# Three weight conversions placed behind the store of the last but one token tile on ScalarE

## The chip, the core and the metric

The kernel runs on one core of a Trainium2 chip. The metric is the device time of one launch in microseconds (us). A core has five engines with an instruction stream each: TensorE (PE, matrix products), VectorE (DVE), ScalarE (ACT), GpSimd (POOL) and SyncE (SP, which here only starts transfers). Each stream is worked off in its own order; an instruction that waits holds up all that stand behind it on its engine. ACT and POOL start transfers as well: ACT stores of plain tiles, POOL gathers and scatters whose rows are named by an index tile.

## The reference, cut to what matters

```python
attn = softmax(masked q k^T) v                  # 2 batches, 8 heads, 768 positions, 64 wide
x  = attn as [1536 tokens, 512]
x2 = ((x @ w_a) * (x @ w_b)) @ w_out            # w_a, w_b [512, 1536], w_out [1536, 512]
logits = x2 @ w_gate                            # 8 experts, 192 tokens each, picked greedily
for e in range(8):
    out[tokens of e] = maximum(x2[tokens of e] @ w1[e], 0) @ w2[e]   # w1 [512, 1024], w2 [1024, 512]
```

## The kernel before

The kernel runs in four stages. Attention comes first, then the gated product G = (x w_a)(x w_b), then x2 = G w_out together with the choice of experts, and then the eight experts one after the other. Matrix products in full precision are made of high and low parts: a value is rounded into a tile `hi` (or `gh`, `ehi`, `xt`), the rest goes into `lo` (`gl`, `elo`), and the products hi·hi, hi·lo and lo·hi are added.

The change sits at the seam between x2 and the experts. `second` makes x2 in 12 tiles of 128 tokens (t = 0 to 11), each from three units of four rows of blocks of G, so 36 units. For a unit, ACT rounds a piece of G into `gh` (L977), POOL subtracts into `gl` (L978), and PE makes twelve products into `px` (L992). There are three buffers of `gh`, so the rounding of unit i + 3 waits until PE is through with unit i. After the third unit of a tile ACT copies `px` into `x2` (L998) and starts its store into the DRAM tensor `x2d` (L999); the last tile (t = 11) is copied into `x2last`.

PE's order is written out by hand in this stage (a `manual_schedule` of PE alone); that of ACT, DVE, POOL and SP is chosen by the scheduler of the framework, and is fixed in the program. In the experts' stage the orders of PE, ACT and DVE are written by hand.

Expert 0 needs its 192 rows of x2. `first_rows` has POOL gather them from `x2d` with two indirect transfers into `first0` (128 rows) and `first1` (64 rows, both L1033). They read the tiles 0 to 10 of `x2d` only; rows of tile 11 come out of `x2last`. PE turns the gathered rows (`begin_rows`, L1050, eight matmuls for each of the two) and adds the rows of tile 11 by a product of `x2last` with a selection tile `ones` (L1162, eight matmuls). ACT and DVE split the result `pt` into the high and low `xt` (L1084, L1085), and the first products `p` of expert 0 follow (L1107, 64 matmuls, then the second products `y`, from L1113 on).

The experts' weights come in 64 chunks of 512 KB (`eraw`, loaded by SP at L1012). `weight_high` rounds a chunk on ACT into `ehi` (L1017) and `weight_low` subtracts on DVE into `elo` (L1022). Chunks 0 to 3 are loaded and converted ahead of the experts. Chunk 0 goes into a pool of its own; chunks 1, 2 and 3 go into a pool, `pre2`, that takes over the room of the routing's tiles, and so its first conversion waits for the routing's last instruction on DVE (`oidx`, L947). Chunks 4 and later go into a pool that takes over the room of the x2 stage.

Of the kernel before, what the change touches and what calls it, by code (L numbers as in the profile page):

```python
# [63 lines left out]
def f32(ap):  # L64
    return ap.bitcast(F32)


class Kernel:
# [500 lines left out]
    def run(self):  # L569
        tc, nc = self.tc, self.nc  # L570
        H, NT, E = self.H, self.NT, self.E
        with ExitStack() as top:
# [107 lines left out]
            def gate(Q, c):  # L680
                assert all(f in done for f in range(4 * Q + 4))
                for j in range(4):
                    f = 4 * Q + j
                    nc.tensor.matmul(pg[c][32 * j:32 * j + 32, :], wp[:, f, :], g_of(f, 512 * c, 512),
                                     start=(Q == 0), stop=(Q == 2), tile_position=(0, 32 * j),
                                     skip_group_check=True)
# [31 lines left out]
            exraw = exs.enter_context(tc.tile_pool(name="exraw", bufs=EXR, side="right"))  # L718
            pre = exs.enter_context(tc.tile_pool(name="pre", bufs=1, side="right"))
# [7 lines left out]
            with tc.manual_schedule(engines={mybir.EngineType.PE}):  # L727
                x2last = pre.tile([128, self.Dm], F32, name="x2last")
                rest = self.second(sec, g_parts, woh, wol, rpsum, x2last)
                left = [36 * NT]  # L730

                def fill(n):
                    for _ in range(n):
                        next(rest, None)
                        left[0] -= 1

                fill(START[0])
                gate(2, 2)
                for c in range(3):
                    nc.scalar.activation(lgT[:, c, :], pg[c], AF.Copy)  # L740
                if "lgT" in self.dbg:
                    nc.sync.dma_start(self.dbg["lgT"], lgT)
                L = self.fold_logits(rpool, rpsum, lgT, fill)
                gpx.close()
                rpq = ExitStack()
                rpp = rpq.enter_context(tc.tile_pool(name="rpq", bufs=1, space=PSUM, side="right"))
                self.routing(rpool, rpsum, rpp, L, lgT.rearrange("p a (b c) -> p (a b) c", c=128), ROUNDS, False, fill)
                rpq.close()
                trp = exs.enter_context(tc.tile_pool(name="trp", bufs=1, space=PSUM, side="right"))
                fill(left[0] - 35)  # L750
                first = self.first_rows(pre, rpool, x2last)
                weights = []
                for c in range(4):
                    if c == 1:
                        rps.close()
                        pre2 = exs.enter_context(tc.tile_pool(name="pre2", bufs=1, side="right"))
                    weights.append(self.weight_high(pre2 if c else pre, self.weight_load(exraw, c), 3 if c else 1))
                    self.weight_low(weights[c])
                fill(10 ** 6)
                rows, last, ones = first  # L760
                pts = [trp.tile([128, 2, self.cap], F32, name="pt", tag="ptr", bufs=2) for _ in range(2)]
                for h in range(2):
                    for k in range(4):
                        self.begin_rows(pts[k // 2][:, k % 2, :], rows, h, k)
# [201 lines left out]
    def second(self, pool, g_parts, woh, wol, ps, x2last):  # L966

        nc = self.nc
        units = [(t, f0) for t in range(self.NT) for f0 in (0, 4, 8)]
        parts, out = {}, {}  # L970

        def split(i):
            t, f0 = units[i]
            gh = pool.tile([128, 4, 128], F32R, name="gh", tag="gh", bufs=3)
            gl = pool.tile([128, 4, 128], F32R, name="gl", tag="gl", bufs=3)
            for fs, src in g_parts(f0, 128 * t):
                nc.scalar.activation(gh[:, fs], src, AF.Copy)  # L977
                nc.gpsimd.tensor_tensor(gl[:, fs], src, f32(gh[:, fs]), op=OP.subtract)  # L978
            parts[i] = gh, gl

        split(0)
        split(1)
        for i, (t, f0) in enumerate(units):
            if i + 2 < len(units):
                split(i + 2)
            gh, gl = parts.pop(i)
            if f0 == 0:
                out[t] = ps.tile([128, 512], F32, name="px2", tag="px2", bufs=2)
            for ff in range(4):
                f = f0 + ff  # L990
                for w, x, n in ((gh, woh, 0), (gh, wol, 1), (gl, woh, 2)):
                    nc.tensor.matmul(out[t], w[:, ff, :], x[f], start=(f == 0 and n == 0), stop=(f == 11 and n == 2))  # L992
                    yield
            if f0 == 8:
                x2 = x2last
                if t + 1 < self.NT:
                    x2 = pool.tile([128, 512], F32, name="x2", tag="x2", bufs=1)
                nc.scalar.activation(x2, out.pop(t), AF.Copy)  # L998
                nc.scalar.dma_start(self.x2d[128 * t:128 * t + 128, :], x2)  # L999


    def weight_load(self, pool, c):
# [348 lines left out]
```

## Time and profile before

| what | value |
|---|---|
| device time, median of 3 runs | 632.42 us (631.93 to 633.57) |
| device time of the profiled execution | 632.53 us |
| span of the profiled execution | 630.5 us, so 2.0 us lie around it |
| mean granted clock of TensorE over the span | 0.989 |
| PE busy | 610.8 us (97%) |
| DVE, ACT, POOL busy | 403.4, 338.8, 177.6 us |

The span is what the profiler saw from the first instruction to the last. Busy times of different engines overlap. [...]

### The profile page before, as it was taken

The numbers are of one execution on the slowest core, as the hardware profiler recorded it, in microseconds if no ns is written. First come the engines' busy times: TensorE is split into PE (matmuls) and PEld (weight loads), VectorE is DVE, ScalarE is ACT, GpSimd is POOL, SyncE is SP. The second block draws the span as 40 slices with busy tenths as digits, with TensorE's granted clock in tenths as the row PEclk, the third lists the DMA queues.
The fourth block names the chain that finished last, engine by engine and source line by source line (L and its number), as shares of the span: only waits on it lengthen the run. The fifth ranks groups of instructions, "written<-read, shape, count | busy, mean of one in ns | idle before, by whom it ended". The sixth has DMA issues, their size and how long they took to land.

```text
span 630.5 us, 10136 instructions
## 1 busy us (share of the span) xinstructions
PE 610.8 (97%) x3645; PEld 479.6 (76%) x3645; DVE 403.4 (64%) x864; ACT 338.8 (54%) x672; POOL 177.6 (28%) x300
## 2 busy tenths in 40 slices
PE   7989999999999999999999999999989999999994
PEld 5667777788877878787867766677778888888883
DVE  6788876679975766431125557666327878778782
ACT  4888777635442433223126655764335866657661
POOL 5658565500000000001024343444421323122221
PEclk9999999999999999999999999999979999999997
DMA  7976320035541433200040000000186788777831
GB/s 159 213 156 150 68 69 2 2 98 170 165 136 34 135 99 101 67 1 0 1 125 25 18 35 18 31 21 19 39 286 190 253 262 270 246 251 223 272 135 34
DMA packets 82603, 72.16 MB, mean 114 GB/s; under 512 B 41073, under 2 KB 69745, under 8 KB 82545
## 3 DMA queue, kind: packets, MB, share of 16 engines
q1 hardware_dynamic: 78704, 61.99, 33.9%
q0 software_dynamic: 2112, 6.30, 3.3%
q10 hardware_dynamic: 1728, 3.15, 1.3%
q8 instruction: 31, 0.51, 0.3%
q14 instruction: 28, 0.22, 0.1%
HBM read 65.13 MB, written 6.29 MB: 113 GB/s over the span
## 4 chain that ended last, share of the span: by engine, by line
PE 81%; issue 9%; POOL 3%; DVE 2%; ACT 2%; DMA 2%; SPq 0%; POOLq 0%; DVEq 0%; ACTq 0%
PE pb L559 14%; PE pa L559 14%; PE px L992 14%; PE p L1107 7%; PE pa L470 4%; PE px L367 4%; PE s L273 3%; PE pa L334 3%; PE pq L871 2%; POOL out_dram L1122 2%; PE y L1113 1%; PE y L1114 1%; PE pt L237 1%; PE y L1118 1%; PE y L1115 1%
## 5 line engine op out<-in xcount | busy, mean ns | idle before, releaser
L1022 DVE TENSOR_TENSOR elo<-eraw,ehi 128x1024 fp32r<-128x1024 f32 x64 | 75.9, 1217 | 5.0 <-ACT ehi L1017 5.0
L1107 PE MATMUL p<-xt,ehi 128*128 128x384 f32 x256 | 73.6, 360 | 0.0
L978 POOL TENSOR_TENSOR gl<-G,gh 128x512 fp32r<-128x512 f32 (+1 forms) x40 | 49.5, 1248 | 68.2 <-ACT gh L977 64.2
L1017 ACT ACTIVATE ehi<-eraw 128x1024 fp32r<-128x1024 f32 x64 | 65.0, 1054 | 3.7 <-DVE oidx L947 2.2
L1107 PE MATMUL p<-xt,elo 128*128 128x192 f32 x256 | 64.7, 254 | 0.0
L992 PE MATMUL px<-woh,gh 128*128 128x512 f32 x144 | 59.5, 413 | 0.0
L279 ACT ACTIVATE A<-sm,negmax 128x264 f32<-128x264 f32 (+1 forms) x96 | 46.9, 490 | 22.3 <-DVE negmax L277 21.2
L978 POOL TENSOR_TENSOR gl<-GE,gh 128x256 fp32r<-128x256 f32 x8 | 7.1, 883 | 182.0 <-ACT gh L977 178.5
L860 DVE TENSOR_SCALAR gt<-lgT,vmax 128x1536 bf16<-128x1536 f32 x40 | 45.5, 1199 | 20.1 <-ACT lgT L835 17.7
L992 PE MATMUL px<-woh,gl 128*128 128x512 f32 x144 | 57.2, 397 | 0.0
L992 PE MATMUL px<-wol,gh 128*128 128x512 f32 x144 | 57.0, 396 | 0.0
L301 POOL TENSOR_SCALAR A<-A,rs 128x256 f32<-128x256 f32 (+1 forms) x96 | 43.2, 469 | 43.5 <-DVE rs L288 23.9
L566 DVE TENSOR_TENSOR G<-asb,pb 128x512 f32<-128x512 f32 x32 | 21.9, 685 | 48.0 <-PE pb L559 48.0
L559 PE MATMUL pb<-xh,whi 128*128 128x512 f32 x128 | 51.7, 404 | 0.0
L1122 POOL DMA_INDIRECT out_dram<-o,oidx x16 | 26.3, 1645 | 90.1 <-ACT o L1131 68.1
L559 PE MATMUL pb<-xh,wlo 128*128 128x512 f32 x128 | 50.1, 392 | 0.0
L559 PE MATMUL pa<-xh,wlo 128*128 128x512 f32 x128 | 50.0, 390 | 0.0
L559 PE MATMUL pb<-xl,whi 128*128 128x512 f32 x128 | 49.9, 390 | 0.0
L559 PE MATMUL pa<-xl,whi 128*128 128x512 f32 x128 | 49.9, 390 | 0.0
L559 PE MATMUL pa<-xh,whi 128*128 128x512 f32 x128 | 49.8, 389 | 0.0
L1107 PEld LDWEIGHTS p<-xt,elo 128*128 128x128 f32 x256 | 49.4, 193 | 0.6 <-ACT xt L1084 0.2
L1107 PEld LDWEIGHTS p<-xt,ehi 128*128 128x128 f32 x256 | 48.3, 189 | 0.7
(224 smaller groups left out, 1418.5 us busy)
## 6 DMA issues: line engine op xcount, KB each, us to landing
eraw<-in_moe_w_dram SPq DMA_DIRECT2D x64, 512.0 KB
wraw<-in_moe_w_a_dram SPq DMA_DIRECT2D x12, 512.0 KB
wraw<-in_moe_w_b_dram SPq DMA_DIRECT2D x12, 512.0 KB
wraw<-in_moe_w_out_dram SPq DMA_DIRECT2D x12, 512.0 KB
x2d<-x ACTq DMA_DIRECT2D x11, 256.0 KB
rawv<-in_v_dram SPq DMA_DIRECT2D x10, 256.0 KB
rawq<-in_q_dram SPq DMA_DIRECT2D x8, 256.0 KB
rawk<-in_k_dram SPq DMA_DIRECT2D x8, 256.0 KB
```

Of the source, the lines that this page charges most:

```text
L279: nc.scalar.activation(st.A2[:, j, h, c0:], sm[:, :n], AF.Exp, bias=self.negmax[:, cc], scale=-1.0, accum_out=self.sums[:, cc])
L301: nc.gpsimd.tensor_scalar(blocks, blocks, st.r2[:, j, h:h + 1], 1.0, op0=OP.mult, op1=OP.mult)
L367: nc.tensor.matmul(px[64 * h:64 * h + 64, cols], vv[:, vcol[h]], st.AT[h][:, sl].rearrange("p a b -> p (a b)"), start=(not g and n == 0), ...
L470: nc.tensor.matmul(p, w[:, k, :], x[c][:, k, :], start=(k == 0 and t == 0), stop=(k == 3 and t == 2))
L559: nc.tensor.matmul(pab[m], w[:, k, :], x[:, k, :], start=(k == 0 and t == 0), stop=(k == 3 and t == 2))
L860: nc.vector.tensor_scalar(gt, vrow, v, None, op0=OP.is_lt)
L978: nc.gpsimd.tensor_tensor(gl[:, fs], src, f32(gh[:, fs]), op=OP.subtract)
L992: nc.tensor.matmul(out[t], w[:, ff, :], x[f], start=(f == 0 and n == 0), stop=(f == 11 and n == 2))
L1017: self.nc.scalar.activation(hi, raw, AF.Copy)
L1022: (eng or self.nc.vector).tensor_tensor(lo, raw, f32(hi), op=OP.subtract)
L1107: nc.tensor.matmul(p1[:, ff, 0:c], w[:, k, cols], x[:, k, 0:c], start=(n == 0), stop=(k == 3), skip_group_check=True)
L1122: st = nc.gpsimd.indirect_dma_start(out=self.out, out_offset=bass.IndirectOffsetOnAxis(ap=self.oidx[:n, 2 * e + h:2 * e + h + 1], axis=0), ...
```

## The change

`second` keeps the instruction that starts the store of a tile; when chunks 1, 2 and 3 are converted, the name `x2store` holds the store of tile 10, the last but one (tile 11 is made after them by `fill(10 ** 6)`). `issue_after` gives each instruction that the block writes on that instruction's engine, which is ACT, a place behind it. It orders them on the engine and adds no wait. The loads of the chunks and the subtractions on DVE are outside of the block.

```diff
                     if c == 1:
                         rps.close()
                         pre2 = exs.enter_context(tc.tile_pool(name="pre2", bufs=1, side="right"))
-                    weights.append(self.weight_high(pre2 if c else pre, self.weight_load(exraw, c), 3 if c else 1))
+                    raw = self.weight_load(exraw, c)
+
+                    with tc.issue_after(self.x2store.ins) if c else ExitStack():
+                        weights.append(self.weight_high(pre2 if c else pre, raw, 3 if c else 1))
                     self.weight_low(weights[c])
...
                 nc.scalar.activation(x2, out.pop(t), AF.Copy)
-                nc.scalar.dma_start(self.x2d[128 * t:128 * t + 128, :], x2)
+                self.x2store = nc.scalar.dma_start(self.x2d[128 * t:128 * t + 128, :], x2)
```

On ACT, at the end of the x2 stage, the rows before are these. `x_4985` is the copy of tile 9 and `x_5072` that of tile 10, the first pair of `gh` after tile 9's store is the first unit of tile 11, and the names in brackets are the engines and transfers that a row waits for.

```order
L999 DMA x2d<-x_4985 128x512 [waits Activation_49]
L977 ACTIVATE gh<-G 128x256 [waits PE_49,Pool_49]
L977 ACTIVATE gh<-G 128x256
L977 ACTIVATE gh<-G 128x512 [waits PE_49,Pool_49]
L1017 ACTIVATE ehi<-eraw 128x1024 [waits DVE_49,PE_49]
L1017 ACTIVATE ehi<-eraw 128x1024 x2
L977 ACTIVATE gh<-G 128x512 [waits PE_49,Pool_49]
L998 ACTIVATE x_5072<-px_4992 128x512 [waits DMAHW2_49,PE_49]
L999 DMA x2d<-x_5072 128x512 [waits Activation_49]
L998 ACTIVATE x2last<-px_5079 128x512 [waits PE_49]
L999 DMA x2d<-x2last 128x512 [waits Activation_49]
```

At the same place of the changed program, whose lines stand three higher from here on:

```order
L1002 DMA x2d<-x_4985 128x512 [waits Activation_49]
L980 ACTIVATE gh<-G 128x256 [waits PE_49,Pool_49]
L980 ACTIVATE gh<-G 128x256
L980 ACTIVATE gh<-G 128x512 [waits PE_49,Pool_49] x2
L1001 ACTIVATE x_5072<-px_4992 128x512 [waits DMAHW2_49,PE_49]
L1002 DMA x2d<-x_5072 128x512 [waits Activation_49]
L1020 ACTIVATE ehi<-eraw 128x1024 [waits DVE_49]
L1020 ACTIVATE ehi<-eraw 128x1024 x2
L1001 ACTIVATE x2last<-px_5079 128x512 [waits PE_49]
L1002 DMA x2d<-x2last 128x512 [waits Activation_49]
```

The three conversions have moved past three rows: the last `gh` (the third unit of tile 11), the copy of tile 10 and its store. Nothing else moves on ACT ahead of the last lines of the program.

On POOL the order is the same in both programs. This is the place where it waits for the stores; `DMAHW` are transfers, among them the eleven stores of the tiles 0 to 10.

```order
L978 TENSOR_TENSOR gl<-G,gh 128x256 [waits PE_49,Activation_49]
L978 TENSOR_TENSOR gl<-G,gh 128x256 [waits Activation_49]
L978 TENSOR_TENSOR gl<-G,gh 128x512 [waits PE_49,Activation_49] x2
L1033 DMA first_5081<-x2d,idx 128x512 [waits DMAHW4_49,DMAHW3_49,DMAHW5_49,DMAHW2_49,DMAHW6_49,DMAHW1_49,DMAHW7_49,DMAHW0_49,DVE_49]
L1033 DMA first_5086<-x2d,idx 64x512
L1066 DMA xe_5196<-x2d,idx 128x512 [waits DMAHW6_49,PE_49,Pool_49]
```

The first gather has the last `gl` ahead of it and waits for the stores; the second stands right behind it. PE, DVE and SP keep their orders too. Instructions that a general path holds for inputs with ties are arranged a little otherwise in the changed program; with these inputs that path is not entered.

## Rows read from the trace of the kernel before

**Rows 1.** Busy time by stretch, with granted clock, DMA share and GB/s.

```profile
core 0: us, PE busy (x) PEld busy (x) DVE busy (x) ACT busy (x) POOL busy (x), PEclk, DMA share, GB/s
43.50:47.60 4.10, 2.83 (x24) 2.08 (x25) 4.03 (x12) 2.76 (x11) 1.99 (x6) 1.00 0.37 112
456.90:460.30 3.40, 1.16 (x8) 0.97 (x8) 0.00 (x0) 0.60 (x1) 0.30 (x1) 1.00 0.81 189
460.30:467.10 6.80, 6.13 (x22) 5.78 (x23) 1.12 (x2) 0.98 (x2) 2.61 (x3) 0.50 1.06 392
```

**Rows 2.** TensorE in order of time: start us, us, engine, line, operation, idle before.

```profile
448.29 0.39 PE L992 MATMUL px<-woh,gl 128*128 128x512 f32 x1
...
456.48 0.39 PE L992 MATMUL px<-woh,gl 128*128 128x512 f32 x1
458.41 1.16 PE L1050 MATMUL pt<-ident,first 128*128 128x128 f32 x8 [1.55 <-DMA first<-x2d,idx]
460.97 1.97 PE L1050 MATMUL pt<-ident,first 64*128 64x64 f32 x8 [1.39 <-DMA first<-x2d,idx]
462.86 2.93 PE L1162 MATMUL pt<-ones,x2last 128*128 128x192 f32 x8
```

**Rows 3.** The chain of waits: start us, us, what.

```profile
451.67 2.02 DMA x2d<-x
...
454.77 1.16 POOL first L1033
...
456.23 4.69 DMA first<-x2d,idx
...
465.79 9.93 PE p L1107 x64
...
486.17 9.08 PE p L1107 x64
```

**Rows 4.** ScalarE in order of time, same columns.

```profile
447.68 2.96 ACT L1017 ACTIVATE ehi<-eraw 128x1024 fp32r<-128x1024 f32 x3 [2.25 <-DVE oidx L947]
450.55 0.61 ACT L977 ACTIVATE gh<-G 128x512 fp32r<-128x512 f32 x1
451.07 0.57 ACT L998 ACTIVATE x<-px 128x512 f32<-128x512 f32 x1
...
456.90 0.60 ACT L998 ACTIVATE x2last<-px 128x512 f32<-128x512 f32 x1 [5.26 <-PE px L992]
...
464.61 0.49 ACT L1084 ACTIVATE xt<-pt 128x384 fp32r<-128x384 f32 x1 [7.11 <-PE pt L1162]
...
469.27 1.05 ACT L1017 ACTIVATE ehi<-eraw 128x1024 fp32r<-128x1024 f32 x1
```

**Rows 5.** VectorE in order of time.

```profile
448.78 3.50 DVE L1022 TENSOR_TENSOR elo<-eraw,ehi 128x1024 fp32r<-128x1024 f32 x3 [1.19 <-ACT ehi L1017]
465.13 0.56 DVE L1085 TENSOR_TENSOR xt<-pt,xt 128x384 fp32r<-128x384 f32 x1 [12.86 <-ACT xt L1084]
...
482.56 2.35 DVE L1022 TENSOR_TENSOR elo<-eraw,ehi 128x1024 fp32r<-128x1024 f32 x2
...
494.48 1.21 DVE L1022 TENSOR_TENSOR elo<-eraw,ehi 128x1024 fp32r<-128x1024 f32 x1
```

**Rows 6.** GpSimd in order of time, three issues of indirect transfers.

```profile
456.23 0.97 POOL L1033 DMA_INDIRECT first<-x2d,idx  x1 [0.30 <-issue]
...
482.32 0.90 POOL L1066 DMA_INDIRECT xe<-x2d,idx  x1 [0.30 <-DVE xt L1085]
...
494.37 2.48 POOL L1122 DMA_INDIRECT out_dram<-o,oidx  x1 [2.21 <-DVE o L1138]
```

**Rows 7.** Line L1033, the two gathers for expert 0: issue to landing.

```profile
DMA to landing us min/median/max: 3.6/4.1/4.7
```

**Rows 8.** Line L1066, the 14 gathers of the other experts: issue to landing.

```profile
DMA to landing us min/median/max: 3.0/3.3/6.6
```

**Rows 9.** PE's longest waits from 466 to 631: us in total, times, longest.

```profile
PEld y L1114 <- DVE elo L1022: 2.5, 7, 0.4
```

## The prediction, made before the changed kernel ran

> **What bounds the kernel now.** I read the page first: PE is busy 97% of the span (the table above), so time can only come from PE's few gaps or from stretches in which PE is busy at the lower clock. [...] The timeline of PE says what it waits for there [rows 2]: the last product of x2 starts at 456.48, then PE is idle 1.55 us until the first gather for expert 0 has landed and 1.39 us until the second has.
>
> The chain of waits says why these are late [rows 3]: the store of tile 10 of x2 is started at 451.67 and lands 2.02 us later, at 453.69; POOL issues the first gather at 454.77, 1.08 us after that landing, and the second at 456.23; it lands 4.69 us later, where PE goes on. ACT's timeline goes one step further back [rows 4]: the copy of tile 10 stands behind the last `gh` with no idle time between, and this behind the three conversions, which sat 2.25 us waiting for the routing's `oidx` and then took 447.68 to 450.55. PE had started the last product of tile 10 at 448.29 [rows 2]. So the store is late by ACT's order alone.
>
> **The change, step by step.** ACT has the same work in another order. The last `gh` and the copy of tile 10 can start when PE is done with tile 10. From the start of the last product to the copy that waits for it is 0.42 us at tile 11 (456.48 to 456.90) [rows 2, 4], so 448.29 becomes 448.71. The copy starts 0.52 us behind the start of `gh` and the store 0.60 us behind the copy, as before (450.55, 451.07, 451.67) [rows 3, 4]: 449.23 and 449.83. The store is 1.84 us earlier. It lands at 451.85, and the first gather is issued 1.08 us later, at 452.93.
>
> The conversions now run from about 449.9 to 452.8. They are needed by products behind 460, and ACT has nothing else until 456.90 [rows 4], so their delay costs nothing on ACT; that idle 5.26 us is their cover. DVE's three subtractions follow the first conversion by 1.10 us (447.68 to 448.78) and take 3.50 us [rows 4, 5]: now about 451.0 to 454.5, nearly three pieces of 1.17 us. They used to be over at 452.28, before the first gather; now both issues of the gathers fall among them.
>
> That is the one new collision, and its price is bounded by two rows [rows 5, 6]. At 494.37 an indirect transfer was issued with a subtraction starting 0.11 us behind it: the issue took 2.48 us instead of some 1.0, and ended 1.16 us after the subtraction did. At 482.32 the subtractions started 0.24 us behind an issue: the issue took 0.90, and the two subtractions their usual 2.35 us. So a subtraction under way can hold an issue, and an issue lets go of DVE early. The first issue at 452.93 meets the second subtraction, which ends at about 453.3: nothing at the low end; at the high end it is held to 453.3 and ends 1.16 us later, at 454.46, against 454.09. The second issue starts 0.30 us behind (as 454.77 + 1.16 to 456.23 [rows 3]): 454.39 or 454.76. If DVE was also held for the whole of the first issue, the third subtraction would run 454.46 to 455.68 and hold the second issue until then; that is the upper bound.
>
> The landing of the second gather before took 4.69 us, that of the first 3.6 [rows 3, 7]. Of the 14 later gathers half took 3.3 or less, 3.0 at least [rows 8]. The loads of the experts' weights, released when PE leaves x2, begin at about 457 and take the DMA engines to a share of 0.81 and then 1.06 [rows 1]; the second gather was caught in that, and now lies mostly ahead of it. I take 3.3 us. The second gather then lands at 454.76 + 3.3 = 458.06 (457.7 without any hold, 459.0 at the upper bound, 459.5 if it is held once and takes 4.69). The first lands at 452.93 + 3.6 = 456.53, or 456.9 if held; PE is free at about 456.71, by the 0.23 us from one such product to the next (36 of them lie between 448.29 and 456.48 [rows 2]). Its eight matmuls took 1.16 us at full clock [rows 2], the tail of the last in it; followed by others I take 1.0 us, up to 457.7 or 457.9. Both gaps shrink to about 0.2 us each.
>
> The clock is the other half. [...] With about 0.4 us it should not fall: from 43.5 to 47.6 us PE was idle 1.27 us of 4.1 and kept 1.00 [rows 1].
>
> The sum on PE, from the start on the second gathered half to the first `y`. Before: 460.97 to 475.72, which is 14.75 us [rows 2, 3]. At full clock: the eight turned rows 1.97 / 2 = 0.98; the eight matmuls with `x2last` 2.85 / 2 = 1.43 (462.94, where the eight before them end, to 462.86 + 2.93 = 465.79) [rows 2]; the 64 products 9.08 instead of 9.93, since those of the next expert took 9.08 at full clock [rows 3]. New is a wait that the low clock hid: the split of `pt` into `xt` takes 0.49 us on ACT and 0.56 on DVE [rows 4, 5], and with PE twice as fast the third and the seventh of the first eight products come before their operand; I follow that chain and get 0.53 us (bounds 0 and 1.05, the two durations together). Together 12.02 us, 2.73 less. The start moves from 460.97 to 458.06, 2.91 less. Sum: 5.64 us.
>
> Nothing behind takes it back. From 466 us on PE's longest kind of wait comes to 2.5 us in seven pieces of at most 0.4 [rows 9], one for each change of expert: one expert follows another at PE's own pace. The next load is that of chunk 4, converted at 469.27 [rows 4] and now at about 463.6. Up to 462 the queues moved 189 GB/s × 3.4 us + 392 GB/s × 1.7 us = 1.31 MB [rows 1]; chunk 4 is the first 0.52 MB of the loads, beside the 0.26 MB of the last store and at most 0.39 MB of the gathers, so I take it as landed by 462. Its slack is some 1.6 us; without that cover, each microsecond it is late is one on ACT, and PE feels it only behind the second pair of products. The tail behind PE's end moves along as it is.
>
> So the profiled 632.53 becomes 626.9. The median of the runs shown, 632.42, lies 0.1 us below the profiled one; I leave 626.9.
>
> **The rivals.** Differences of under 0.3%, 1.9 us, I call no change; that is about what a measurement of this kernel can tell.
>
> *The port holds in both directions.* The second gather's issue waits for the third subtraction, and lands at 459.0 to 459.5. For it: the 2.48 us issue. Against it: the subtractions behind the 482.32 issue were not held. Saved then are 2.73 + 1.97 to 1.47, so 4.7 to 4.2: 627.8 to 628.3. [...]
>
> *The clock falls anyway.* PE still has small gaps, and what counts as busy for the granted clock the rows do not tell. For it: two gaps of 1.5 us were enough before. Against it: the 43.5 stretch. Then only the 2.91 us of the earlier start remain: 629.6.
>
> *It does nothing.* The copy would have to be held by something that the timeline hides behind the conversions, or the first gather by something else than the store. Against it: `gh` has no idle time before it, and its other waits (a buffer that PE frees, POOL's `gl`) were past. 632.5.
>
> *Slower.* If both issues took 2.48 us and the second landed as long behind its issue's end as before (4.69 − 0.97 = 3.72 [rows 3, 6]), it would land at 452.93 + 2.48 + 0.30 + 2.48 + 3.72 = 461.91, 0.94 us later than PE went on before, with the clock lost as before: 633.5. It decides from where the second issue ends after 457.2, its end before. Against it: there is no subtraction left on DVE after about 455.7.
>
> **How the numbers follow.** The forecast (saved 5.0 to 6.5, so 626.0 to 627.5) gets 0.63, the port 0.14, the clock 0.11, nothing 0.08, slower 0.04. The low end is no hold, so that PE goes on at 457.72, and no wait for `xt`: 3.25 + 2.73 + 0.53 = 6.5 below 632.42, 625.9, less 0.2 for the spread of runs. The high end takes in the port and the clock: 629.8. Faster by over 0.3% are the first three, 0.88; of the last two, both within 1.9 us as priced, 0.03 stay for slower by more.
>
> **What would show it.** The store of tile 10 at about 449.8 and the first gather's issue at 452.9; that issue between 1.0 and 1.6 us long; PE's two gaps at 456.9 and 459.6 gone or under 0.3 us; a granted clock of 1.00 from 456 to 470; the first `y` of expert 0 at about 470.1 instead of 475.72; the conversion of chunk 4 without a wait for its load. The forecast is wrong if the second issue is over 2 us long, if the clock shows 0.50 in any stretch before the end, or if the first gather waits for something that ends at 453.7 as before.

## The result, and the profile after

The changed kernel takes 628.3 us (median of 6 runs, 626.88 to 630.47) against 634.05 us before (6 runs, 631.93 to 635.31). The ratio is 0.9915, 95% interval 0.9887 to 0.9942, so 5.4 us less (3.7 to 7.2). The profiled execution took 627.70 us, 4.83 us less than the profiled one of before.

ScalarE of the changed kernel in order of time answers to [rows 4]:

```profile
448.57 0.63 ACT L980 ACTIVATE gh<-G 128x512 fp32r<-128x512 f32 x1 [3.12 <-PE px L995]
449.11 0.58 ACT L1001 ACTIVATE x<-px 128x512 f32<-128x512 f32 x1
...
450.09 2.96 ACT L1020 ACTIVATE ehi<-eraw 128x1024 fp32r<-128x1024 f32 x3 [0.40 <-ACT x L1001]
456.92 0.60 ACT L1001 ACTIVATE x2last<-px 128x512 f32<-128x512 f32 x1 [3.87 <-PE px L995]
...
464.03 1.05 ACT L1020 ACTIVATE ehi<-eraw 128x1024 fp32r<-128x1024 f32 x1
```

The last `gh` now waits for PE instead of standing behind the conversions, and the copy of tile 10 starts 1.96 us earlier. ACT still idles ahead of `x2last`, and the conversion of chunk 4 has no wait for its load. GpSimd and VectorE answer to [rows 5, 6]:

```profile
452.82 1.75 POOL L1036 DMA_INDIRECT first<-x2d,idx  x1 [2.25 <-DVE elo L1025]
454.88 0.97 POOL L1036 DMA_INDIRECT first<-x2d,idx  x1 [0.30 <-issue]
```

```profile
451.19 3.50 DVE L1025 TENSOR_TENSOR elo<-eraw,ehi 128x1024 fp32r<-128x1024 f32 x3 [3.58 <-ACT ehi L1020]
```

The first issue falls into the second of three subtractions and takes 1.75 us instead of 1.16; the second starts 0.31 us behind its end, as before, by when the third subtraction is over (454.69), and takes 0.97 as before. The second gather from issue to landing (the view pairs this one of the two):

```profile
DMA to landing us min/median/max: 3.2/3.2/3.2
```

TensorE answers to [rows 2], the chain of waits to [rows 3], the stretches to [rows 1], with their columns:

```profile
456.50 0.39 PE L995 MATMUL px<-woh,gl 128*128 128x512 f32 x1
456.98 2.22 PE L1053 MATMUL pt<-ident,first 128*128 128x128 f32 x16
459.13 1.57 PE L1165 MATMUL pt<-ones,x2last 128*128 128x192 f32 x8
```

```profile
452.82 4.11 DMA first<-x2d,idx
...
461.28 9.21 PE p L1110 x62
470.49 0.25 PE y L1116
```

```profile
456.90:460.30 3.40, 3.32 (x23) 3.11 (x24) 0.00 (x0) 0.76 (x2) 0.00 (x0) 1.00 0.52 175
460.30:467.10 6.80, 6.68 (x45) 6.21 (x44) 2.93 (x7) 3.83 (x7) 3.11 (x4) 1.00 1.07 388
```

Both gaps are gone: all 16 matmuls on the gathered rows run in one piece, and from 456.9 to 460.3 us PE is busy 3.32 us where it was 1.16. From 460.3 to 467.1 us the granted clock, a share of TensorE's full speed, is 1.00 where it was 0.50 [rows 1]. Counted from the start of the last product of x2 to the first `y`, the seam takes 470.49 − 456.50 = 13.99 us; before it took 475.72 − 456.48 = 19.24 us [rows 2, 3]. It is 5.25 us shorter, beside a timed gain of 5.4.

I compare experiments by this length of the seam, because the time at which x2 ends differs from execution to execution, by some 3 us, for reasons ahead of the seam (last section).

### The profile page after: what moved, and what is told of

The parts are those of the page before. It is cut to its first block, busy times and chain, and to the rows that moved or that the text cites. A ratio compares the mean times of both kernels' runs of the same rounds, so it can differ in the third digit from the quotient of the medians.

```text
span 625.6 us, 10135 instructions
## 1 busy us (share of the span) xinstructions
PE 608.3 (97%) x3645; PEld 477.0 (76%) x3645; DVE 403.3 (64%) x864; ACT 339.0 (54%) x672; POOL 178.5 (29%) x300
## 4 chain that ended last, share of the span: by engine, by line
PE 81%; issue 9%; POOL 2%; DVE 2%; DMA 2%; ACT 2%; SPq 0%; POOLq 0%; DVEq 0%; ACTq 0%
PE pb L559 14%; PE px L995 14%; PE pa L559 14%; PE p L1110 7%; PE pa L470 4%; PE px L367 4%; PE s L273 4%; PE pa L334 3%; PE pq L874 2%; POOL out_dram L1125 2%; PE y L1116 1%; PE y L1117 1%; PE pt L237 1%; PE y L1121 1%; PE y L1118 1%
```

## The experiments

| kernel | seam in its profile, us | granted clock in it | timed ratio to before (95%) |
|---|---|---|---|
| before | 19.24 | falls to 0.50 | |
| before, second profile | 19.13 | falls to 0.50 | |
| changed | 13.99 | 1.00 | 0.9915 (0.9887 to 0.9942) |
| changed, second profile (after_again) | 13.98 | 1.00 | 0.9920 (0.9901 to 0.9939) |
| fill_gaps | 17.26 | 1.00 | 0.9965 (0.9951 to 0.9980) |
| hold_loads | 15.42 | 1.00 | 0.9966 (0.9951 to 0.9981) |
| hold_loads, second profile (hold_again) | 18.03 | falls to 0.50 | |
| late1 | 15.91 | falls to 0.50 for 3.4 us | 0.9926 (0.9903 to 0.9948) |
| late1, second profile | 15.95 | falls to 0.50 for 3.4 us | |
| late2 | 19.00 | falls to 0.50 | 0.9988 (0.9971 to 1.0004) |
| late2_fill | 16.48 | 1.00 | 0.9958 (0.9942 to 0.9973) |
| late3 | 20.07 | falls to 0.50 | 1.0023 (1.0006 to 1.0040) |
| spread | 13.74 | 1.00 | 0.9920 (0.9898 to 0.9942) |

Two of the expectations below name seams of 15.26 us (hold_loads) and 15.74 us (late1); by the measure of this table they are 15.42 and 15.91.

**The clock alone: fill_gaps.** It is the kernel before with spare matmuls on PE ahead of the gathered rows; their result is read by nobody.

```diff
+                spare = rpsum.tile([128, 512], F32, name="px2", tag="px2", bufs=2)
                 for h in range(2):
+                    for _ in range((7, 6)[h]):
+                        nc.tensor.matmul(spare.rearrange("p (a b) -> p a b", a=4), self.rc[1],
+                                         self.rc[1].unsqueeze(1).to_broadcast([128, 4, 128]), start=True, stop=True)
                     for k in range(4):
```

> The kernel before, with 7 and 6 spare 512-column matmuls on PE in the two gaps ahead of the gathered rows; the store and the gathers stay as late as before. Theory (two halves: an earlier start, and a clock that fell because PE had no work): granted clock 1.00 through the seam, first y of expert 0 at about 473.0 instead of 475.72, time 2.7 us below the kernel before. Rival 1 (the clock falls for another reason, or the low clock costs nothing there): no change against before, 475.7. Rival 2 (the spare matmuls delay the gathered rows by themselves): up to 0.4 us of the gain is lost.

TensorE of fill_gaps in order of time, and its gathers from issue to landing (the view pairs one of the two here, the second):

```profile
458.54 0.39 PE L996 MATMUL px<-woh,gl 128*128 128x512 f32 x1
458.77 1.68 PE L765 MATMUL px<-onesb 128*128 128x512 bf16 x7
460.45 1.16 PE L1054 MATMUL pt<-ident,first 128*128 128x128 f32 x8
```

```profile
DMA to landing us min/median/max: 5.0/5.0/5.0
```

The store and the gathers were as late as before, and the seam still got 1.98 us shorter (timed: 0.35% of 633.76, 2.2 us). Rival 1 falls: with PE kept at work the clock was 1.00 in both stretches behind x2, from 458.9 to 469.2 us. Rival 2 took nothing, as PE still waited 0.51 us for the second gather behind the spare matmuls. The 2.7 us that I expected were not reached in full for two reasons: the second gather took 5.0 us instead of 4.69, so that PE went on with it 0.37 us later than before (4.86 us from the start of the last product instead of 4.49), and from there to the first `y` it took 12.40 us, not 12.02. Before it was 14.75, so the clock was worth 2.35 us.

**The store's time alone: late1, late2, late3.** The changed kernel, with the copy of tile 10 written two, three or four times over, so that only its store and what hangs on it move back; the conversions keep their place behind it.

```diff
-                nc.scalar.activation(x2, out.pop(t), AF.Copy)
+                for _ in range(3 if t == self.NT - 2 else 1):
+                    nc.scalar.activation(x2, out[t], AF.Copy)
+                del out[t]
```

> The changed kernel with the copy of tile 10 made three times over instead of once, so that the store of tile 10 starts about 1.2 us later while the last gh and the conversions keep their new order. Theory (the store's time is what counts): first gather issued at about 454.1, PE idle 1.2 to 1.5 us ahead of the first gathered rows, start on the second half at 459.3 to 460.3; if the clock stands that gap, 1.2 to 2.2 us above the changed kernel, if not, 4 to 5 us above it. Rival (the gain came from the last gh and gl, or from the conversions being out of the way, not from the store): no change against the changed kernel.

> As late2, with the copy of tile 10 made four times: the store starts about 1.9 us later, where it was before the change. Theory: both gaps of PE and the low clock come back, first y of expert 0 at 475.7 to 476.5, time equal to the kernel before or up to 0.8 us above it (the issue of the first gather is still held by the subtractions, as it was not before). Rival (not the store): no change against the changed kernel.

> The changed kernel with the copy of tile 10 made twice, so that its store starts about 0.6 us later. In late2 1.3 us of delay moved the first y by 5.0 us, counted from the start of the last product of x2 (13.99 us in the changed kernel, 19.00 in late2, 19.24 before). Theory (the delay itself, plus two steps: the second gather meeting the loads of the weights, and the clock): with one PE gap of 0.7 to 0.9 us the clock stands, and the second gather is issued 1.0 us ahead of the end of x2; 14.6 us if it lands ahead of the loads, up to 15.9 if it meets them. Rival (the price grows in proportion to the delay): 16.5 us.

TensorE of late2 in order of time, and the two stretches behind its x2 (columns as in [rows 1]):

```profile
457.53 0.39 PE L995 MATMUL px<-woh,gl 128*128 128x512 f32 x1
459.30 1.16 PE L1055 MATMUL pt<-ident,first 128*128 128x128 f32 x8 [1.38 <-DMA first<-x2d,idx]
461.74 1.97 PE L1055 MATMUL pt<-ident,first 64*128 64x64 f32 x8 [1.29 <-DMA first<-x2d,idx]
```

```profile
457.90:461.30 3.40, 1.18 (x9) 0.97 (x8) 0.00 (x0) 0.60 (x1) 0.24 (x1) 0.98 0.74 195
461.30:468.20 6.90, 6.46 (x24) 6.11 (x25) 1.11 (x2) 0.98 (x2) 2.85 (x3) 0.52 1.06 388
```

The rival of late2 and late3 is refuted: with `gh` and the conversions in their new places, the time goes back as the store goes back. late3, with the store where it was, is 0.83 us worse at the seam than before; the second issue started 0.54 us later against x2's last product than before, behind the held first one, and its landing took 5.1 us instead of 4.69. Timed it is 1.5 us (0.4 to 2.5) worse. But the price is no straight line: store delays of 0.65, 1.26 and 1.92 us, counted against x2's last product, lengthened the seam by 1.92, 5.01 and 6.08. In late2 1.3 us of delay cost 5.0 us: the gap, a second gather that landed 4.5 us behind its issue at 457.17, and the clock. I had not reckoned with that landing: with x2 1.0 us later than in the changed kernel, the second half started at 461.74, not at 459.3 to 460.3. In late1 I expected the clock to stand one gap of 0.84 us, and in both of its profiles it fell:

```profile
457.94 0.39 PE L995 MATMUL px<-woh,gl 128*128 128x512 f32 x1
459.17 2.19 PE L1055 MATMUL pt<-ident,first 128*128 128x128 f32 x16 [0.84 <-DMA first<-x2d,idx]
461.29 2.77 PE L1167 MATMUL pt<-ones,x2last 128*128 128x192 f32 x8
```

The gathered rows ran in one piece, at full clock, and the eight matmuls behind them, 1.57 us long in the changed kernel, took 2.77. The seam came to 15.9 us instead of 14.6. That is the 15.9 that I had set for a second gather that meets the loads, but for another reason: it did not meet them (3.1 us to landing), it was the clock. The proportional rival's 16.5 was not reached either. Timed it is 4.7 us (3.3 to 6.2) below before, and not every execution seems to have lost the clock. Two of the six took 628.27 and 628.29 us at a mean granted clock of 0.996 over the span, as in the changed kernel's profile; 3.4 us at 0.50 would take 0.003 off that. The times say the same: the fastest of 12 executions of the changed kernel, 626.88 us, and the 1.92 us of late1's seam make 628.8. The trace of these two was not kept, so this is inferred.

**Delay and clock apart: late2_fill.** late2 with the spare matmuls of fill_gaps.

> late2 with the 7 and 6 spare matmuls of fill_gaps in PE's gaps. Theory: the clock stays at 1.00, which is worth 2.0 to 2.4 us, and the late second gather stays: 16.6 to 17.0 us from the last product of x2 to the first y instead of 19.00. Rival (nearly all of late2's 5.0 us is the clock, the landing would be made up elsewhere): about 14.5 us.

16.48 us and 1.00 throughout the seam, 2.52 us less than late2. Of these, 2.40 lie behind the start on the second half (14.79 us from there to the first `y` in late2, 12.39 here), which is the clock; that start itself came 0.12 us earlier against x2's last product. So about half of late2's 5.01 us is the clock and the rest is delay. The rival, all of it the clock, falls.

**The loads alone: hold_loads.** The kernel before, with a wait of SP for the second gather put ahead of the loads of chunks 4 and later.

```diff
                 first = self.first_rows(pre, rpool, x2last)
+                mark = dram.tile([1, self.Dm], F32, name="mark")
+                self.landed = nc.sync.dma_start(mark, first[0][1][0][0:1, :])
...
             for c in range(4, 4 + EARLY):
-                load(c)
+                with tc.issue_after(self.landed.ins) if first else ExitStack():
+                    load(c)
```

> The kernel before, with one row of the second gather stored to DRAM by SP ahead of the loads of chunks 4 and later, so that these loads start only when that gather has landed (and 2 to 3 us later than before). Theory (the second gather took 4.69 us instead of 3.2 because it met these loads): it lands 3.0 to 3.3 us behind its issue, PE's second gap of 1.39 us shrinks to under 0.2; with the clock lost as before the first y comes 1.2 to 1.5 us earlier from the last product of x2 (17.8 to 18.0 us), with the clock kept 3.6 us earlier (15.6). Rival (gathers of 64 rows behind another are slow by themselves): 4.7 us again, 19.2 us or more.

> hold_loads once more. Its first profile kept the clock over one gap of 1.5 us (15.26 us to the first y), but its timed median is only 2.2 us below the kernel before instead of 3.8. Theory (with a single gap the clock is kept in some executions and lost in others): 15.3 or 16.5 to 17.7 us; either is possible, and a loss here would show the chance. Rival (kept always, and the timed difference has another source): 15.3 us.

The gathers of hold_loads from issue to landing, and TensorE in order of time in the first and the second profile of the program:

```profile
DMA to landing us min/median/max: 3.2/3.4/3.5
```

```profile
459.68 0.39 PE L994 MATMUL px<-woh,gl 128*128 128x512 f32 x1
461.60 2.21 PE L1052 MATMUL pt<-ident,first 128*128 128x128 f32 x16 [1.53 <-DMA first<-x2d,idx]
463.74 1.57 PE L1165 MATMUL pt<-ones,x2last 128*128 128x192 f32 x8
```

```profile
457.84 0.39 PE L994 MATMUL px<-woh,gl 128*128 128x512 f32 x1
459.69 2.72 PE L1052 MATMUL pt<-ident,first 128*128 128x128 f32 x16 [1.46 <-DMA first<-x2d,idx]
462.34 2.93 PE L1165 MATMUL pt<-ones,x2last 128*128 128x192 f32 x8
```

With the loads held, the second gather lands 3.2 us behind its issue in both profiles, although it was issued as late as before, and PE's second gap is gone. It had met the loads; by itself this gather of 64 rows is not slow. The other profiles say how close was too close here. SP issued the first of the loads 0.52 us behind the start of x2's last product in before and in the changed kernel (457.00 and 457.02); with that figure for the other runs, an estimate, the second gather took 4.4 to 5.1 us to land where the loads began 0.2 to 0.9 us behind its issue (before, before_again, fill_gaps, late2, late3), and 3.1 or 3.2 where they began 1.5 or 2.1 us behind it (late1, the changed kernel). And the same program kept the clock in one execution over a gap of 1.53 us and lost it in the other over one of 1.46: 2.61 us between the two seams. The timed gain, 2.2 us (1.2 to 3.1), lies between what either of them would give, 1.21 and 3.82, though its interval just reaches the smaller.

**The hold of the issue: spread.** The changed kernel with the three conversions in three places.

```diff
+                    if c == 3:
+                        fill(10 ** 6)
-                    with tc.issue_after(self.x2store.ins) if c else ExitStack():
+                    with tc.issue_after(self.x2store.ins) if c > 1 else ExitStack():
                         weights.append(self.weight_high(pre2 if c else pre, raw, 3 if c else 1))
                     self.weight_low(weights[c])
-                fill(10 ** 6)
```

> The changed kernel with the conversion of chunk 1 free to go ahead of the last gh, that of chunk 2 behind the store of tile 10, that of chunk 3 behind the store of tile 11, so that no subtraction is under way when the gathers are issued. Theory (the hold of the issue by a subtraction is the only new cost, 0.75 us on the issue, of which PE feels the part ahead of the end of x2): first issue about 1.0 us long, PE goes from x2 to the gathered rows without a gap, first y of expert 0 about 0.2 to 0.5 us earlier than in the changed kernel. Rival (the issue is long for another reason): issue 1.75 us as in the changed kernel, no change. A subtraction of chunk 3 that now meets the split into xt on VectorE would cost up to 0.5 us.

GpSimd and TensorE of spread in order of time:

```profile
453.87 1.16 POOL L1037 DMA_INDIRECT first<-x2d,idx  x1 [1.73 <-DVE elo L1026]
455.33 0.97 POOL L1037 DMA_INDIRECT first<-x2d,idx  x1 [0.30 <-issue]
```

```profile
457.43 0.39 PE L996 MATMUL px<-woh,gl 128*128 128x512 f32 x1
457.66 2.08 PE L1054 MATMUL pt<-ident,first 128*128 128x128 f32 x16
```

With no subtraction under way the first issue takes 1.16 us again, and PE goes from x2 to the gathered rows in the 0.23 us of its own pace. The seam is 0.25 us shorter than in the changed kernel, too little for the timed ratio to tell (0.9920 beside 0.9915 and 0.9920). The subtraction of chunk 3 now ends at 461.47, and the split behind it makes PE wait 0.28 us; that eats part of it.

**Second profiles.**

> The changed kernel once more, for a second profile. Theory: 13.9 to 14.1 us from the last product of x2 to the first y, clock 1.00 through the seam, whatever the time of the execution; a time other than the first profile's by 1 to 2 us would show in TensorE's clock ahead of 60 us, as it did in late2 and late3. Rival (the clock at the seam is won only in some executions): 0.50 at the seam, some 16.4 us.

> The kernel before once more, for a second profile of the clock at the seam. Theory (gaps of 1.55 and 1.39 us right behind one another lose the clock in nearly every execution): 0.50 for 6.8 us, 19.1 us from the last product of x2 to the first y. Rival (the clock there is a matter of chance in each execution): 1.00 or a shorter stretch at 0.50, 16.7 to 18 us.

> late1 once more. Its first profile lost the clock for 3.4 us behind a gap of 0.8 us (15.74 us to the first y), its timed median is 4.7 us below the kernel before instead of 3.3. Theory (chance from execution to execution): 14.5 us with the clock kept, 15.7 with it lost. Rival (0.8 us is always enough to lose it): 15.7 us.

The changed kernel showed the same seam to 0.01 us, the kernel before the same to 0.11, with the clock lost both times. For late1 the rival's 15.7 us, a gap of 0.8 us that always loses the clock, came in both profiles (15.9 by the table); the two fast timed executions named above speak against the "always".

## Why the prediction was right

**The step on ACT** came as worked out. The copy started at 449.11 (forecast 449.23) and the first issue at 452.82 (452.93). late1 to late3 show that the store's time is what counts. One sign was missed: the first issue took 1.75 us, not 1.0 to 1.6.

**The landing.** The first gather landed at 456.93, where the chain of waits goes through and PE goes on (forecast 456.53, or 456.9 if held). The landing of the second came at 454.88 + 3.2 = 458.08; the forecast was 458.06. That it was so close owes something to two errors against each other: the hold of the first issue was 0.59 us beyond its 1.16, not 0.37, because the conversions started 0.4 us behind the store's issue, not 0.1, and the second subtraction so ended later; and the landing took 3.2 us, not 3.3. That the landing is shorter than 4.69 us once the loads begin well behind the issue is shown by hold_loads, where holding the loads did the same for a gather that was not moved.

**The clock** was kept in both profiles of the changed kernel. That lost work on PE was the cause of its fall is shown by fill_gaps and late2_fill: 1.00 with spare matmuls in the gaps, where before and late2 show 0.50 and 0.52 without them. My argument for why it would be kept was too simple: I set a stretch with 1.27 us of idle time against the new 0.4 us, as if less idle time were safe. late1 lost the clock over 0.84 us. hold_loads kept it once over 1.53. The forecast held because the two gaps shrank to 0.1 us in the profile's busy time, not because a known bound was kept; so far it was luck.

**The sum.** From the landing to the first `y` the forecast was 12.02 us, measured 470.49 − 458.08 = 12.41. The term that was off is the new wait for `xt`: taking the 64 products at 9.08 and the eight matmuls ahead of them at 1.43 us from 459.13, it is 470.49 − 9.08 − 460.56 = 0.85 us instead of 0.53, within its bounds of 0 and 1.05. So the clock's half was worth 14.75 − 12.41 = 2.34 us (forecast 2.73), the earlier start 460.97 − 458.08 = 2.89 (2.91), together 5.23 (5.64). fill_gaps and late2_fill put the clock at 2.35 and 2.40. The experiments divide the gain in their own way: hold_loads in its second profile is 1.21 us better than before by the loads alone; the clock kept gives another 2.61; from there to the changed kernel the rest of the earlier store gives 15.42 − 13.99 = 1.43; together 5.25.

**Behind the seam** PE took nothing back: its last product starts at 615.96 instead of 621.20, 5.24 us earlier. The tail did not quite move along as it was: from there to the end of the span it is 9.6 us instead of 9.3, which is most of what the profiled times (4.83 us apart) lack to the seam's 5.25.

**The rivals.** By the port in both directions the prediction means that an issue holds the subtractions as they hold it. That did not come: the third subtraction did not wait for the first issue, which ended at 454.57, and was over, at 454.69, before the second issue began at 454.88. The first issue was held while a subtraction was under way (1.75 us, and 1.16 in spread, where none was), but the three subtractions took their usual 3.50 us across that issue, so here the hold was one-sided. What holds the issue, a port or something else, no run shows. The clock that falls anyway did not come in the changed kernel, but late1 shows how near it was: 0.6 us later at the store, and in its profiles 1.9 us of 5.25 were gone. Nothing and slower are refuted by the times.

**The level.** 628.3 lies 1.4 us above the forecast 626.9, but so does the median of the runs of before in the later measurement, by 1.6 us above the one that was shown. Taken by itself it lies outside the 626.0 to 627.5 that got 0.63 and at the end of the port's 627.8 to 628.3, but the rows above rule the port out; the difference to before, 5.4 us by the ratio, is close to the 5.6 forecast.

## What to carry to other kernels

Where two engines meet at a seam, look for what the in-order engine in between has ahead of the one instruction that starts the transfer: three conversions that nobody needed for 10 us cost 5 us there. Two things made small delays expensive here: a gather issued 0.2 to 0.9 us ahead of a burst of loads, which took 4.4 to 5.1 us to land instead of 3.1 or 3.2, and a gap of PE over which the clock fell to 0.50 (0.84 us in late1, 1.46 in the second profile of hold_loads). With both, 1.3 us at the store cost 5.0 us at the first product. So a gain that is read as a shift of 2 us can be worth more than twice that, and a harmless-looking 0.6 us can take a third of it back.

## What the runs showed of the hardware that was not expected

The clock at one gap is not the same from execution to execution: hold_loads kept 1.00 over 1.53 us without work and fell to 0.50 over 1.46. Which of them comes is not told by the length of the gap, and no run here settles what tells it.

The start of the kernel varies as well. The stretches from 0 to 60 us, of the changed kernel and of late1, belong to the same part of the program, which no edit touched:

```profile
0.00:60.00 60.00, 53.55 (x427) 38.81 (x428) 46.46 (x177) 42.96 (x136) 36.93 (x107) 1.00 0.82 178
```

```profile
0.00:60.00 60.00, 53.55 (x413) 39.30 (x415) 45.54 (x174) 41.71 (x132) 35.61 (x102) 0.91 0.81 173
```

At a mean granted clock of 0.91 instead of 1.00 fewer instructions were done in that time (413 matmuls instead of 427), and x2's last product started 1.4 us later (457.94 against 456.50). In the ten other profiles of these experiments it started between 456.68 and 459.68. The recorded clock does not tell all of this. In fill_gaps it is 1.00 from 0 to 60 us, and yet PE did only 407 matmuls there in 54.37 us of busy time, 0.134 us each, where the changed kernel did 427 in 53.55, 0.125 us each, and x2's last product came at 458.54. late3, where it came at 458.57, has a mean granted clock of 0.992 over the span; a drop from 0 to 60 us like that of late1 would by itself take some 0.009 off it, so by this estimate late3 had none, though after_again's expectation takes it for an example of one. So a granted clock is best checked against the length of a matmul. At the seam the two agree: the eight matmuls with `x2last` took 1.57 us in the changed kernel, fill_gaps, hold_loads, late2_fill and spread, where the table says 1.00, and 2.77 to 2.93 in before, late1, late2 and the second profile of hold_loads, where it falls. Differences of up to 3.2 us from the stages ahead of the seam are more than some of the differences tested here, beside a spread of 1.4 to 4.8 us among the runs of one kernel; the length of one stage within a profile is the sharper measure.

An indirect transfer's issue that falls into a subtraction on VectorE took 1.67 to 1.75 us in the changed kernel, late2 and late3 instead of 1.16, and the subtractions lost nothing (three took 3.50 us in each, as in before).
